# An attention and two-expert-layer kernel: `w_out`'s conversion, the gate products and the late logits placed later in attention, and the gate's weights loaded at another step

## The chip, the cores and the metric

The kernel runs on one core of a Trainium2 chip. The metric is the device time of one execution in microseconds (us); a smaller time is better. A core has a matrix engine (TensorE, PE in the profile, with its weight loads as PEld), a vector engine (VectorE, DVE), an activation engine (ScalarE, ACT), a general engine (GpSimd, POOL) and a queue engine (SyncE, SP) that issues most transfers. Each works through its own instructions in order and waits for the others by semaphores. Sixteen DMA engines move data between HBM and the on-chip memory.

## The reference, cut to what matters

Multi-head attention with normalized q and k, then a dense layer with an ELU between two matrices, then a layer of eight experts with a greedy assignment of tokens.

```python
# attention: 4 batches, 12 heads, 448 rows, 64 columns a head
q_n, k_n = rmsnorm(q, g_q), rmsnorm(k, g_k)
attn = softmax(scale * q_n @ k_n.T)
x = concat_heads(attn @ v)                 # 1792 x 768
# dense layer: w_in 768 x 2048, w_out 2048 x 768
h = x @ w_in
g = where(h > 0, h, exp(min(h, 0)) - 1)
x = g @ w_out
# experts: w_gate 768 x 8, w1 8 x 768 x 1024, w2 8 x 1024 x 768
logits = x @ w_gate
...                                        # greedy: best (token, expert) first, at most 224 a expert
for e in range(8):
    out[mask_e] = relu(x[mask_e] @ w1[e]) @ w2[e]
```

`w_in` and `w_out` come as 64-bit floats, the other inputs as 32-bit floats.

## The kernel before

Every product is made of 16-bit pieces: a matrix is split into a high and a low half, and three matmuls (high by high, low by high, high by low) stand for one. The logits must be exact enough to order the tokens, so they are not taken from `x @ w_gate` after the second matrix but from `g` by the product of `w_out` and `w_gate`, called `Wg` here, which the kernel makes itself.

Attention goes over 24 pairs of heads (4 batches of 6 pairs), two pairs (a `Duo`) being loaded, normalized and transposed together. For each pair PE makes scores (`ps`), DVE their maxima (`sm`), ScalarE the exponentials (`pe`), GpSimd scales them, PE transposes them (`pta`, `ptb`) and multiplies them by v (`po`); ScalarE and DVE then write the two halves of the result into `xT` (lines 578 and 579).

Beside attention run other streams of work. `w_in` is converted from 64-bit floats (`load_steps`, lines 369 to 383: three DVE operations into `cv`, two on ScalarE, one on GpSimd). The hidden layer of a finished batch (`hidden`, line 665) has 16 blocks of 18 matmuls (`ph`), each followed by the ELU and two stores of `g` to HBM (`g_d`, `gt_d`). `w_out` is converted in 16 blocks (`gate_products`, line 602): each block `wo` is stored to HBM (`wo_d`), transposed by two DMA transposes (`wt`), and PE multiplies it by the gate's weights (`pw`, 12 short matmuls), which gives 128 rows of `Wg`. The logits of batches 2 and 3 are made from `g` while it is on the chip; those of batches 0 and 1 (`late_logits`, line 653) need `g` from HBM again: four blocks of `g` are loaded into four buffers (`gl`), and PE adds their logits (`pl`, a group of 8 matmuls). After attention the hidden layer of the last batch and the second matrix (`py`) follow, with `w_out` loaded from `wo_d`, then the assignment of tokens, woven with the rest of the second matrix, and then the experts.

The order of the streams is written by time steps. A pair has 16 steps, so attention has 384 and its loads begin at step -48. `at(t, f)` puts a piece of attention at step t. A `Spread(gen, n, t0, t1)` takes n pieces from a generator at an even pace from step t0 to step t1. After that the framework's scheduler orders the instructions of each engine by its own estimate of time, from the dependencies and this order; the built order of both programs is therefore quoted below. The lines that the change touches are the last two spreads and the step of `load_gate`:

```python
Spread(gate_products(), NG, 180, 280),
Spread(chain_gens(late_logits(b) for b in range(LB)), 2 * LB * NF // LG, 295, 400),
...
at(-30, load_gate)
```

Names: `wg` are the gate's weights, `acc` the logits' sums, `st` the landing buffers of weights (three), `wo` has two buffers, `wt` three, `gl` four, and `pt` in PSUM has three that `pta`, `ptb`, `po`, `pw` and `pl` share.

Of the kernel before, what the change touches and what calls it, by code (L numbers as in the profile page):

```python
# [8 lines left out]
F16 = mybir.dt.float16  # L9
# [246 lines left out]
def kernel(  # L256
# [14 lines left out]
    nc = tc.nc  # L271
    PE, ACT, DVE, POOL = nc.tensor, nc.scalar, nc.vector, nc.gpsimd

    B, H, S, D = q.shape
# [5 lines left out]
    P = 128  # L280
    NP = H // 2
    KC = DM // P
    NF = FF // P
# [3 lines left out]
    MAIN = NJ * P  # L287
    TAIL = S - MAIN
# [33 lines left out]
    def mm(o, l, r, key=None, **kw):  # L322

        i = PE_mm(o, l, r, **kw)  # L324
        if key is not None:
            if key in last_in_bank:
                tc.add_manual_dep(i.ins, last_in_bank[key].name, NOSYNC, reason="order in a bank")
            last_in_bank[key] = i.ins
        return i
# [6 lines left out]
    g_d = [dram.tile([P, NF, 2, MAIN], F16, name=f"g_d{b}") for b in range(B)]  # L336

    gt_d = [dram.tile([P, NF, 2, 2 * TAIL], F16, name=f"gt_d{b}") for b in range(B // 2)]
# [18 lines left out]
    def load_steps(hi, lo, src):  # L357

        w = src.shape[1]
        if src.dtype == F32:  # L360
            st = stg.tile([P, w], F32, tag="st", name="st")
            i = nc.sync.dma_start(st, src)
            if hold:
                tc.add_manual_dep(i.ins, hold[-1].ins.name, NOSYNC, reason="not before its turn")
            split(hi, lo, st, w)
            yield
            return

        for a in range(0, w, 512):
            n = min(512, w - a)  # L370
            st = stg.tile([P, n, 2], I32, tag="st", name="st")
            nc.sync.dma_start(st.rearrange("p n t -> p (n t)"), src[:, a:a + n].bitcast(I32))
            cv = gat.tile([P, n], I32, tag="cv", bufs=3, name="cv")
            i = DVE.tensor_scalar(cv, st[:, :, 1], 3, 0x3FFFFFF8, op0=ALU.logical_shift_left, op1=ALU.bitwise_and)
            if pace:
                tc.add_manual_dep(i.ins, pace[-1].ins.name, NOSYNC, reason="not before its turn")
            DVE.scalar_tensor_tensor(cv, st[:, :, 1], -0x40000000, cv, op0=ALU.bitwise_and, op1=ALU.bitwise_or)  # L377
            DVE.scalar_tensor_tensor(cv, st[:, :, 0], 29, cv, op0=ALU.logical_shift_right, op1=ALU.bitwise_or)  # L378
            cf = cv.bitcast(F32)
            ACT.activation(cf, cf, AF.Copy, scale=SW)  # L380
            ACT.copy(hi[:, a:a + n], cf)
            POOL.tensor_sub(lo[:, a:a + n], cf, hi[:, a:a + n])
            yield
# [13 lines left out]
    def key():  # L397
        n_key[0] += 1
        return n_key[0]
# [4 lines left out]
    gat = att_s.enter_context(tc.tile_pool(name="gat", bufs=2))  # L404
# [3 lines left out]
    psT = ps1.enter_context(tc.tile_pool(name="psT", bufs=3, space=PSUM))  # L408
# [188 lines left out]
    def load_gate():  # L597
        nc.sync.dma_start(wg32, w_gate.rearrange("(c p) e -> p c e", p=P))
        ACT.activation(wg16[:, :, 0:NE], wg32, AF.Copy, scale=-SW)
        DVE.scalar_tensor_tensor(wg16[:, :, NE:], wg32, -SW, wg16[:, :, 0:NE], op0=ALU.mult, op1=ALU.subtract)  # L600

    def gate_products():
        wts = None
        for f in range(NF):
            wo = gat.tile([P, 2, DM], F16, name="wo")
            yield from load_steps(wo[:, 0, :], wo[:, 1, :], w_out[f * P:(f + 1) * P, :])
            if f:
                gate_product(f - 1, wts)
                yield
            nc.sync.dma_start(wo_d[:, f], wo)  # L610
            wts = []
            for z in range(2):
                wts.append(gat.tile([P, KC, P], F16, name="wt", bufs=3))
                nc.sync.dma_start_transpose(wts[z], wo[:, z, :])
            yield
        gate_product(NF - 1, wts)
        yield

    def gate_product(f, wts):
        pw = psT.tile([P, 2 * NE], F32, tag="pt", name="pw")  # L620
        for z in range(2):
            n = NE if z else 2 * NE
            for c in range(KC):
                mm(pw[:, 0:n], wts[z][:, c, :], wg16[:, c, 0:n], start=(z == 0 and c == 0),
                   stop=(z == 1 and c == KC - 1), skip_group_check=True)
        t = gat.tile([P, NE], F32, name="wgt")
        ACT.copy(t, pw[:, NE:])
        DVE.tensor_add(t, t, pw[:, 0:NE])
        DVE.tensor_copy(Wg[:, f, 0:NE], t)
        DVE.tensor_copy(Wg[:, f, WG:], t)  # L630
        DVE.tensor_sub(Wg[:, f, NE:2 * NE], t, Wg[:, f, 0:NE])

    LG = 4

    def logits(pool, tag, b, gs):

        pl = pool.tile([P, S], F32, tag=tag, name="pl")
        kk = key()
        for i, (g, f) in enumerate(gs):
            for z, (o, n) in enumerate(((0, WG), (WG, NE))):  # L640
                mm(pl[o:o + n], Wg[:, f, o:o + n], g[:, z, :], key=kk,
                   start=(i == 0), stop=(i == len(gs) - 1), skip_group_check=True)
        n = WG + NE
        for o, w, c in ((b * MAIN, MAIN, 0), (B * MAIN + b * TAIL, TAIL, MAIN)):
            a = acc[:, o:o + w]
            if gs[0][1] == 0:
                DVE.tensor_copy(a, pl[0:n, c:c + w])
            else:
                DVE.tensor_add(a, a, pl[0:n, c:c + w])

    LB = 2

    def late_logits(b):
        for f in range(0, NF, LG):
            gs = []
            for i in range(f, f + LG):
                gl = gat.tile([P, 2, S], F16, bufs=LG, name="gl")
                nc.sync.dma_start(gl[:, :, 0:MAIN], g_d[b][:, i])
                nc.sync.dma_start(gl[:, :, MAIN:S], gt_d[b // 2][:, i, :, b % 2 * TAIL:(b % 2 + 1) * TAIL])
                gs.append((gl, i))  # L660
            yield
            logits(psT, "pt", b, gs)
            yield

    def hidden(b, xT):

# [28 lines left out]
        if b >= LB:  # L695
            logits(psT, "pt", b, gs[NF - LG:NF])
# [14 lines left out]
    def chain_gens(gens):  # L711
        for g in gens:
            yield from g

    def w_in_steps(u):
        for c in range(KC):
            load_w_in(u, c)
            yield
# [5 lines left out]
    def at(t, f, *a):  # L724
        todo.setdefault(t, []).append((f, a))

    NG = NF * (2 + DM // 512 + 1)
    spreads = [
        Spread(w_in_steps(0), KC, 40, 96),
        Spread(chain_gens(w_in_steps(i) for i in range(1, FF // WB)), KC * (FF // WB - 1), 96, 176),  # L730
        Spread(gate_products(), NG, 180, 280),
        Spread(chain_gens(late_logits(b) for b in range(LB)), 2 * LB * NF // LG, 295, 400),
    ]
    at(-47, load_gain)
    at(-30, load_gate)
    NSTEP = B * SEQ
    for b in range(B):
        xT = big.tile([P, KC, 2, S], F16, name="xT")
# [122 lines left out]
    for o in range(0, NCH, h):  # L861
        pt = psR.tile([P, h, n], F32, tag=f"rt_pb{4 if o else 0}", name="plt")
# [152 lines left out]
```

## Time and profile before

| | |
|---|---|
| time, median of 3 runs | 1150.81 us (1146.79 to 1153.8) |
| the profiled execution | 1149.89 us, its span 1148.2 us |
| PE busy in the span | 1037.0 us (90%) |
| DVE | 787.0 us (69%) |
| ACT | 538.5 us (47%) |
| POOL | 354.1 us (31%) |
| mean granted TensorE clock | 0.968 of full speed |

The profile is one execution. Busy time is the time in which an engine had an instruction at work, so instructions that overlap are counted once, and a matmul that runs at the lower clock counts with its longer time. The share over the whole span is a mean over stages with different limits: attention ends about 540 us after the span's start, the second matrix and the assignment of tokens follow to about 880, then the experts. The table by stretch is the view that tells the stages apart.

### The profile page before, as it was taken

Reading aid. Unit: us, or ns where it says so; the run is one execution under the profiler, and the core shown is the slowest. Engines: PE = TensorE matmul, PEld = TensorE weight load, DVE = VectorE, ACT = ScalarE, POOL = GpSimd, SP = SyncE. Lnnn points to the kernel's source line nnn. Section 1 sums busy time; section 2 is a strip of 40 time slices with the busy share of each in tenths; the row PEclk is TensorE's granted clock in tenths of the full one; section 3 lists DMA queues with packets and bytes.
Section 4 is the critical chain, followed back from the end, with each engine's and each line's share of the span. In section 5 each row is a group of like instructions: output and inputs, shape, how many; then the busy total and the mean of one; then the engine's idle time right before and its main releaser. Section 6 shows DMA issues by size and latency. Waiting matters only on the chain.

```text
span 1148.2 us, 19348 instructions
## 1 busy us (share of the span) xinstructions
PE 1037.0 (90%) x7030; PEld 608.9 (53%) x7030; DVE 787.0 (69%) x1567; ACT 538.5 (47%) x1099; POOL 354.1 (31%) x462
## 2 busy tenths in 40 slices
PE   0687879897989989999999999999999799999997
PEld 0233434443544444444444545555546688888885
DVE  3798898999988775654334778887786556666620
ACT  2676677776867765554441111011112455555510
POOL 3677686657756542221001000000000412222100
PEclk9977889999999999999999999999999899999999
DMA  6355575559998736334922151131133778777710
GB/s 173 80 123 130 136 206 164 152 162 246 259 246 207 193 74 135 97 80 148 398 78 69 59 196 59 49 132 49 49 104 100 238 244 247 255 252 255 239 41 25
DMA packets 190319, 176.48 MB, mean 154 GB/s; under 512 B 114704, under 2 KB 161808, under 8 KB 189456
## 3 DMA queue, kind: packets, MB, share of 16 engines
q1 hardware_dynamic: 186064, 163.78, 49.7%
q0 software_dynamic: 3328, 11.01, 3.0%
q8 instruction: 55, 0.90, 0.3%
q10 hardware_dynamic: 832, 0.46, 0.1%
q14 instruction: 40, 0.33, 0.1%
HBM read 125.92 MB, written 31.98 MB: 138 GB/s over the span
## 4 chain that ended last, share of the span: by engine, by line
PE 51%; DVE 18%; DMA 11%; issue 10%; ACT 5%; POOL 3%; SPq 2%; POOLq 0%; DVEq 0%; ACTq 0%
PE py L324 18%; PE ph L324 11%; DMA st<-in_moe_w_dram 4%; PE pye L324 4%; PE po L324 4%; PE phe L324 3%; DVE sm L533 2%; PE ps L324 2%; PE rt_pc L324 2%; DVE cv L377 2%; PE pta L324 2%; DMA qn<-in_q_dram 2%; PE pl L324 1%; DVE cv L378 1%; DVE rt_C L127 1%
## 5 line engine op out<-in xcount | busy, mean ns | idle before, releaser
L324 PE MATMUL ph<-xT,w_in 128*128 128x448 f16 x1152 | 247.2, 359 | 7.8 <-DVE elu_g L685 4.8
L324 PE MATMUL py<-w_out,g 128*128 128x384 f16 x1152 | 203.8, 328 | 0.0
L324 PEld LDWEIGHTS <-w_in 128*128 128x128 f16 x1152 | 108.0, 99 | 125.4 <-issue 44.7
L545 POOL TENSOR_SCALAR pe<-pe,sm 128x448 f32<-128x448 f32 x168 | 127.0, 766 | 141.0 <-DVE sm L541 78.9
L351 DVE SCALAR_TENSOR_TENSOR w<-st,w 128x768 f16<-128x768 f32 (+1 forms) x112 | 119.4, 1073 | 72.1 <-ACT w L350 65.8
L324 PEld LDWEIGHTS <-g 128*128 128x128 f16 x1152 | 107.3, 98 | 81.4 <-issue 18.5
L350 ACT ACTIVATE w<-st 128x768 f16<-128x768 f32 (+1 forms) x112 | 103.8, 933 | 89.3 <-DMA st<-in_moe_w_dram 84.0
L324 PE MATMUL ps<-kT,qT 64*128 64x448 f16 (+1 forms) x576 | 94.3, 382 | 54.5 <-ACT pe L535 29.2
L535 ACT ACTIVATE pe<-ps,sm 128x448 f32<-128x448 f32 x168 | 105.7, 633 | 50.1 <-DVE sm L533 47.6
L324 PE MATMUL pye<-w,hT 128*112 128x512 f16 (+1 forms) x768 | 126.4, 326 | 0.0
L127 DVE TENSOR_SCALAR rt_C<-rt_row,rt_m 128x1792 f16<-128x1792 f32 x98 | 107.3, 1149 | 8.2 <-PE rt_pc L324 7.4
L533 DVE TENSOR_REDUCE sm<-ps 128x1 f32<-128x448 f32 x168 | 100.2, 614 | 17.8 <-PE ps L324 15.5
L324 PEld LDWEIGHTS <-w 128*128 128x128 f16 x1152 | 110.4, 99 | 3.3 <-DVE xTe L922 1.2
L324 PE MATMUL phe<-xTe,w 128*128 128x224 f16 x1080 | 109.2, 261 | 2.1 <-DVE xTe L922 1.1
L324 PEld LDWEIGHTS <-hT 128*112 128x112 f16 x768 | 91.6, 130 | 32.1
L815 ACT ACTIVATE xh<-py 128x384 f16<-128x384 f32 x28 | 13.7, 490 | 176.6 <-PE py L324 159.2
L324 PEld LDWEIGHTS <-qT 64*128 64x128 f16 (+1 forms) x576 | 27.5, 100 | 99.0 <-issue 65.9
L324 PE MATMUL pta<-id,pe 128*128 128x128 f32 x384 | 65.3, 293 | 12.7 <-POOL pe L545 4.7
L685 DVE SCALAR_TENSOR_TENSOR elu_g<-ph,elu_e 128x448 f32<-128x448 f32 x64 | 39.6, 618 | 48.0 <-ACT elu_e L683 47.7
L972 POOL DMA_INDIRECT out_dram<-yo,idx x16 | 18.5, 1155 | 173.9 <-DVE yo L971 172.3
L324 PEld LDWEIGHTS pta<-id,pe 128*128 128x128 f32 x384 | 46.1, 148 | 43.1 <-POOL pe L545 16.0
L201 POOL MEMSET rt_c<- 128x8 f16 x8 | 0.9, 123 | 210.1 <-DVE rt_c L207 206.0
(176 smaller groups left out, 1475.1 us busy)
## 6 DMA issues: line engine op xcount, KB each, us to landing
st<-in_moe_w_dram SPq DMA_DIRECT2D x48, 512.0 KB
st<-in_moe_w_dram SPq DMA_DIRECT2D x64, 384.0 KB
st<-in_moe_w_in_dram SPq DMA_DIRECT2D x24, 512.0 KB
g_d<-gt SPq DMA_DIRECT2D x64, 192.0 KB
g<-g_d SPq DMA_DIRECT2D x16, 768.0 KB
st<-in_moe_w_out_dram SPq DMA_DIRECT2D x16, 512.0 KB
gl<-g_d SPq DMA_DIRECT2D x32, 192.0 KB
wo_d<-wo SPq DMA_DIRECT2D x16, 384.0 KB
```

What stands on the lines that cost most here:

```text
L127: i = DVE.tensor_scalar(C.rearrange("p c t -> p (c t)"), row, m[:, s:s + 1], None, op0=ALU.is_le)
L324: i = PE_mm(o, l, r, **kw)
L350: ACT.activation(hi, st, AF.Copy, scale=SW)
L351: DVE.scalar_tensor_tensor(lo, st, SW, hi, op0=ALU.mult, op1=ALU.subtract)
L377: DVE.scalar_tensor_tensor(cv, st[:, :, 1], -0x40000000, cv, op0=ALU.bitwise_and, op1=ALU.bitwise_or)
L378: DVE.scalar_tensor_tensor(cv, st[:, :, 0], 29, cv, op0=ALU.logical_shift_right, op1=ALU.bitwise_or)
L533: i = DVE.tensor_reduce(out=st[:, 0, u:u + 1], in_=ps[u], axis=AX.X, op=ALU.max, negate=True)
L535: ACT.activation(p[:, u, :], ps[u], AF.Exp, bias=st[:, 0, u:u + 1], accum_out=st[:, 1, u:u + 1])
L545: POOL.tensor_scalar(p[:, u, :], p[:, u, :], st[:, 2, u:u + 1], 1.0, op0=ALU.mult, op1=ALU.mult)
L685: DVE.scalar_tensor_tensor(gf, ph, -SG / SH, e, op0=ALU.mult, op1=ALU.min)
L815: ACT.activation(xh[:, 0], py, AF.Copy, scale=-SX2 / (SG * SW))
L972: st = POOL.indirect_dma_start(out=out, out_offset=bass.IndirectOffsetOnAxis(ap=idx[:, 1, 2 * e + hh:2 * e + hh + 1], axis=0), in_=yo, in_ ...
```

## The change

The conversion of `w_out` with the gate products is spread over steps 240 to 368 in place of 180 to 280. The late logits are spread over steps 285 to 400 in place of 295 to 400, and their loop is turned: for each group of four blocks first batch 0, then batch 1, where before all groups of batch 0 came first. So logits are taken from a part of `Wg` while the rest is still being made; a list `ready` and an assertion, which cost nothing on the chip, hold that the order is right. `load_gate` moves from step -30 to step 100.

```diff
--- before.py
+++ after.py
@@ -599,13 +599,15 @@
         ACT.activation(wg16[:, :, 0:NE], wg32, AF.Copy, scale=-SW)
         DVE.scalar_tensor_tensor(wg16[:, :, NE:], wg32, -SW, wg16[:, :, 0:NE], op0=ALU.mult, op1=ALU.subtract)
 
+    ready = []
+
     def gate_products():
-        wts = None
         for f in range(NF):
             wo = gat.tile([P, 2, DM], F16, name="wo")
             yield from load_steps(wo[:, 0, :], wo[:, 1, :], w_out[f * P:(f + 1) * P, :])
             if f:
                 gate_product(f - 1, wts)
+                ready.append(f - 1)
                 yield
             nc.sync.dma_start(wo_d[:, f], wo)
             wts = []
@@ -614,6 +616,7 @@
                 nc.sync.dma_start_transpose(wts[z], wo[:, z, :])
             yield
         gate_product(NF - 1, wts)
+        ready.append(NF - 1)
         yield
 
     def gate_product(f, wts):
@@ -634,6 +637,7 @@
 
     def logits(pool, tag, b, gs):
 
+        assert gs[-1][1] in ready
         pl = pool.tile([P, S], F32, tag=tag, name="pl")
         kk = key()
         for i, (g, f) in enumerate(gs):
@@ -650,17 +654,18 @@
 
     LB = 2
 
-    def late_logits(b):
+    def late_logits():
         for f in range(0, NF, LG):
-            gs = []
-            for i in range(f, f + LG):
-                gl = gat.tile([P, 2, S], F16, bufs=LG, name="gl")
-                nc.sync.dma_start(gl[:, :, 0:MAIN], g_d[b][:, i])
-                nc.sync.dma_start(gl[:, :, MAIN:S], gt_d[b // 2][:, i, :, b % 2 * TAIL:(b % 2 + 1) * TAIL])
-                gs.append((gl, i))
-            yield
-            logits(psT, "pt", b, gs)
-            yield
+            for b in range(LB):
+                gs = []
+                for i in range(f, f + LG):
+                    gl = gat.tile([P, 2, S], F16, bufs=LG, name="gl")
+                    nc.sync.dma_start(gl[:, :, 0:MAIN], g_d[b][:, i])
+                    nc.sync.dma_start(gl[:, :, MAIN:S], gt_d[b // 2][:, i, :, b % 2 * TAIL:(b % 2 + 1) * TAIL])
+                    gs.append((gl, i))
+                yield
+                logits(psT, "pt", b, gs)
+                yield
 
     def hidden(b, xT):
 
@@ -728,11 +733,11 @@
     spreads = [
         Spread(w_in_steps(0), KC, 40, 96),
         Spread(chain_gens(w_in_steps(i) for i in range(1, FF // WB)), KC * (FF // WB - 1), 96, 176),
-        Spread(gate_products(), NG, 180, 280),
-        Spread(chain_gens(late_logits(b) for b in range(LB)), 2 * LB * NF // LG, 295, 400),
+        Spread(gate_products(), NG, 240, 368),
+        Spread(late_logits(), 2 * LB * NF // LG, 285, 400),
     ]
     at(-47, load_gain)
-    at(-30, load_gate)
+    at(100, load_gate)
     NSTEP = B * SEQ
     for b in range(B):
         xT = big.tile([P, KC, 2, S], F16, name="xT")
```

On ACT, at the start of the program (`sq` squares of q and k, `wg` the gate's weights, `ln` and `rs` the normalizing factors, `h` the cast halves, `pe` the first exponentials), before:

```order
L451 ACTIVATE sq<-qn 128x896
L599 ACTIVATE wg_99<-wg_98 128x6x8
L451 ACTIVATE sq<-kn 128x896
L459 ACTIVATE ln<-ss,eps 128x28
L461 ACTIVATE rs<-ln 128x28
L480 CAST h_180<-kn 128x896
L480 CAST h_186<-qn 128x896
L535 ACTIVATE pe,sm<-ps,sm 128x448
```

and changed:

```order
L451 ACTIVATE sq<-qn 128x896
L451 ACTIVATE sq<-kn 128x896
L459 ACTIVATE ln<-ss,eps 128x28
L461 ACTIVATE rs<-ln 128x28
L480 CAST h_177<-kn 128x896
L480 CAST h_183<-qn 128x896
L599 ACTIVATE wg_99<-wg_98 128x6x8
L535 ACTIVATE pe,sm<-ps,sm 128x448
```

The gate's weights moved from the second place to the one ahead of the first exponential.

On DVE, in a late pair of attention, before (`elu_g` and `gt` belong to the hidden layer, `acc` to the late logits):

```order
L533 TENSOR_REDUCE sm<-ps 128x1 x2
L685 SCALAR_TENSOR_TENSOR elu_g<-ph,elu_e 128x448
L540 TENSOR_SCALAR sm<-sm 128x2
L541 RECIPROCAL sm<-sm 128x2
L649 TENSOR_TENSOR acc<-acc,pl 40x384
L649 TENSOR_TENSOR acc<-acc,pl 40x64
L688 TENSOR_TENSOR gt<-elu_g,gt 128x448
L560 COPY PT<-ptb 128x3x128
```

and changed:

```order
L377 SCALAR_TENSOR_TENSOR cv<-st,cv 128x512
L579 SCALAR_TENSOR_TENSOR xT<-po,xT 128x448
L541 RECIPROCAL sm<-sm 128x2
L651 COPY acc<-pl 40x384
L651 COPY acc<-pl 40x64
L541 RECIPROCAL sm<-sm 128x1
L378 SCALAR_TENSOR_TENSOR cv<-st,cv 128x512
L533 TENSOR_REDUCE sm<-ps 128x1
L374 TENSOR_SCALAR cv<-st 128x256
L533 TENSOR_REDUCE sm<-ps 128x1
L560 COPY PT<-ptb 128x3x128
L377 SCALAR_TENSOR_TENSOR cv<-st,cv 128x256
```

The conversion's operations (`cv`) now stand among those of the late logits, which they had all left behind before.

On SP, around a group of loads of late logits, before:

```order
L440 DMA vn_4909<-in_v_dram 128x4x192
L658 DMA gl_5378<-g_d0_76 128x2x384
L659 DMA gl_5378<-gt_d0_80 128x2x64
L658 DMA gl_5381<-g_d0_76 128x2x384
L659 DMA gl_5381<-gt_d0_80 128x2x64
L658 DMA gl_5384<-g_d0_76 128x2x384
L689 DMA g_d2_78<-gt_5275 128x2x384
L690 DMA gt_d1_81<-gt_5275 128x2x64
```

and changed:

```order
L663 DMA gl_4462<-g_d1_77 128x2x384
L664 DMA gl_4462<-gt_d0_80 128x2x64
L612 DMA wo_d_84<-wo_4358 128x1536
L616 DMA_TRANSPOSE wt_4480<-wo_4358 128x6x128
L616 DMA_TRANSPOSE wt_4482<-wo_4358 128x6x128
L372 DMA st_4700<-in_moe_w_out_dram 128x1024
L372 DMA st_4730<-in_moe_w_out_dram 128x512
L372 DMA st_4854<-in_moe_w_out_dram 128x1024
L663 DMA gl_4757<-g_d0_76 128x2x384
L664 DMA gl_4757<-gt_d0_80 128x2x64
L663 DMA gl_4760<-g_d0_76 128x2x384
L616 DMA_TRANSPOSE wt_4662<-wo_4517 128x6x128
```

The store and the transposes of `wo` and the loads of `w_out` now share SP's order with the loads of late logits; before, only stores of `g` and loads of v stood between these.

## Rows read from the trace of the kernel before

**Rows 1.** ACT's copies into `xT`: start us, us; ends of pairs 9, 13, 16, 23.

```profile
235.89 0.54 ACT L578 ACTIVATE xT<-po 128x448 f16<-128x448 f32 x1
330.27 0.54 ACT L578 ACTIVATE xT<-po 128x448 f16<-128x448 f32 x1
407.19 0.53 ACT L578 ACTIVATE xT<-po 128x448 f16<-128x448 f32 x1
538.59 0.54 ACT L578 ACTIVATE xT<-po 128x448 f16<-128x448 f32 x1 [3.45 <-PE po L324]
```

**Rows 2.** Busy time of each engine in stretches A and B.

```profile
core 0: us, PE busy (x) PEld busy (x) DVE busy (x) ACT busy (x) POOL busy (x), PEclk, DMA share, GB/s
235.89:407.19 171.30, 152.95 (x1000) 76.18 (x999) 152.04 (x361) 123.62 (x302) 103.96 (x126) 0.97 0.88 222
407.19:538.59 131.40, 127.13 (x779) 61.99 (x780) 79.69 (x193) 74.61 (x182) 36.14 (x58) 1.00 0.39 93
```

**Rows 3.** PE's waits in stretch A: us in total, times, longest us.

```profile
PE ps L324 <- ACT pe L535: 8.5, 7, 3.2
PE pw L324 <- DMA wt<-wo: 1.1, 2, 0.8
```

**Rows 4.** PE's longest wait in stretch B.

```profile
PE ps L324 <- ACT pe L535: 1.8, 2, 1.1
```

**Rows 5.** The chain that ended last, in stretch A: transposes of `wo`.

```profile
335.90 5.14 DMA wt<-wo
...
360.83 3.58 DMA wt<-wo
...
388.89 2.45 DMA wt<-wo
```

**Rows 6.** Busy time by stretch: pairs 12, 13 and 14, 15, 16, and after attention.

```profile
280.48:303.92 23.44, 18.61 (x130) 10.12 (x130) 22.78 (x58) 16.05 (x42) 16.50 (x16) 0.85 0.99 253
303.92:359.69 55.77, 51.72 (x328) 24.93 (x327) 50.85 (x118) 41.06 (x101) 33.11 (x44) 0.97 0.97 250
359.69:383.50 23.81, 20.16 (x138) 10.49 (x138) 20.57 (x53) 18.60 (x47) 13.36 (x17) 1.00 0.73 191
383.50:407.19 23.69, 21.91 (x162) 11.40 (x159) 15.86 (x43) 14.73 (x37) 12.57 (x18) 1.00 0.83 180
540.00:560.00 20.00, 18.52 (x98) 8.67 (x97) 7.07 (x14) 8.78 (x15) 0.00 (x0) 1.00 0.98 406
```

**Rows 7.** The program's start in order of time: ScalarE, DVE and GpSimd.

```profile
11.44 0.23 DVE L315 SCALAR_TENSOR_TENSOR gain<-gain,gk_b 128x64 f32<-128x64 f32 x1 [1.58 <-DMA gk_b<-in_g_k_dram]
11.77 0.24 ACT L599 ACTIVATE wg<-wg 128x48 f16<-128x48 f32 x1 [3.03 <-DMA wg<-in_moe_w_gate_dram]
11.90 2.07 POOL L454 TENSOR_TENSOR qn<-qn,gain 128x896 f32<-128x896 f32 x1 [8.40 <-DMA vn<-in_v_dram]
11.92 0.95 ACT L451 ACTIVATE sq<-kn 128x896 f32<-128x896 f32 x1
12.04 1.99 DVE L600 SCALAR_TENSOR_TENSOR wg<-wg,wg 128x48 f16<-128x48 f32 x1 [0.38 <-ACT wg L599]
13.96 1.07 DVE L452 TENSOR_REDUCE ss<-sq 128x14 f32<-128x896 f32 x1
...
15.53 0.21 POOL L465 TENSOR_SCALAR ss<-ss 128x28 f32<-128x28 f32 x1 [1.56 <-ACT ln L459]
```

**Rows 8.** The chain that ended last: PE's pieces, start us, us, and their count.

```profile
357.74 0.39 PE pw L324 x12
...
538.54 1.62 PE pl L324 x15
...
549.57 3.52 PE ph L324 x18
...
565.17 0.93 PE py L324 x5
```

**Rows 9.** SP's longest wait in stretch B.

```profile
SPq L658 <- PE pl L324: 32.6, 8, 9.8
```

## The prediction

> **What bounds the kernel now.** I read the page first: its rows by slices show TensorE (PE) at nine tenths in most slices, so one has to look by stage. The moved work lies in attention, and I cut attention at the copies of its 24 head pairs into `xT`, counted from 0 [rows 1]. Pair 10 begins at 235.89 us, where conversion of `w_out` sets in; pair 16, the last that converts, ends at 407.19; the last pair ends at 538.59. The table of busy time by stretch [rows 2] then has two regimes. Stretch A (pairs 10 to 16, 171.30 us) has PE busy 152.95 us and VectorE (DVE) 152.04, both 89%, with the DMA engines at 0.88. Stretch B (pairs 17 to 23, 131.40 us) has PE busy 127.13 us, 97%, with DVE at 79.69 and DMA at 0.39. PE is idle 18.35 us in A (10.7%) and 4.27 us in B (3.2%). So B is bound by PE, and A by a mesh of DVE, DMA and PE. The waits say how A loses its time: PE's scores wait 8.5 us for ScalarE's exponentials in A [rows 3] and 1.8 in B [rows 4]; ScalarE and DVE work in order, and a conversion step that waits holds up what attention needs. The chain that ended last runs in A through the transposes of `wo` [rows 5], 2.5 to 5.1 us a time. Pair 12 stands out [rows 6]: 23.44 us, PE busy 18.61, granted clock 0.85.
>
> All of the possible gain in attention is therefore these 22.6 us of idle PE, and what the clock cost: A's mean is 0.97 against 1.00 in B, so some 3% of 152.95, 4.6 us, was lost at the lower of the two levels.
>
> **Start.** Before, ScalarE's second activation of the program waits 3.03 us for the gate's weights, ahead of the squares of `kn`, and on DVE the correction of these weights takes 1.99 us ahead of the sums of `kn` [rows 7]. The built order shows where they go: not to step 100, but just behind the first two casts of q and k, still ahead of the first exponential; the load goes behind three `w_in` loads on SP. So the words of the change promise more than the program does. DVE can start the sum of `kn` once `gain` is done at 11.67 rather than at 13.96, 2.3 us earlier. What is late next is GpSimd: its `qn` by `gain` ends at 13.97, and the Newton steps, which began at 15.53, can begin then: 1.6 us earlier. I take -1.6. Bounds: -2.3, if that product too runs faster without the DVE instruction beside it, and -0.5, if the correction (0.2 to 2 us on DVE) now delays the first maximum.
>
> **The bulk: pairs 10 to 23.** Up to the middle of pair 10 both programs have the same order on PE and DVE. I counted the instructions by pair in the two orders and gave them the pace of the chain [rows 8]: 3.52 us for 18 `ph`, 0.196 each; 0.39 us for 12 `pw`; 1.62 us for 15 `pl`. Stretch A holds 360 `ph` (70.4 us) and 192 `pw` (6.2); the other 76.3 us are attention, 10.9 a pair. Changed, pairs 10 to 13 hold 181 `ph` and no `pw`: 35.4 + 43.6 = 79.0 us of PE work. All of pairs 10 to 23 is 152.95 + 127.13 = 280.1 us plus 15 `ph` that the new order draws in from behind attention (2.9 us), 283.0. So 204.0 us are left for pairs 14 to 23, with all conversion, all products and seven of the eight groups of late logits.
>
> Pairs 10 to 13 resemble B: no conversion, DVE light. At B's 3.2% idle they last 79.0/0.968 = 81.6 us; before, with conversion and five `ph` more, they lasted 94.4, to 330.27 [rows 1]. For pairs 14 to 23 the idle share decides, and the trace has no such stretch. Nearest rows: B's 3.2% from below, A's 10.7% from above, and between them pairs 13 and 14 [rows 6], which are like the new pairs in having much PE work beside the conversion: 55.77 us, PE busy 51.72, 7.3% idle. I take 7.3%, the row that is nearest: 204.0/0.927 = 220.1 us. Two things speak for less than A: a block of `w_out` comes every 12 us of PE work instead of 9.6 (192.5 us in pairs 14 to 22, and 153, over 16 blocks), and DMA work of about 202 us (0.88 of 171.30 and 0.39 of 131.40) is spread more evenly. One speaks against: DVE's 231.7 us of both stretches less some 47 for pairs 10 to 13 (0.61, B's share, of 77) leaves 0.84 to 0.88 of the new stretch, nearly A's 0.89.
>
> Sum: 81.6 + 220.1 = 301.7 us against 302.70, so -1.0. Ends: 210.7 us at 3.2% gives -10.4; 228.4 us at 10.7% gives +7.3.
>
> **Tail.** The 15 `ph` are missing behind attention: -2.9 us. `w_out` comes back from HBM there, and the first product with it follows the last pair's end after 26.6 us [rows 8], now after some 23.6; the cover is the hidden layer's matmuls, and in 20 us of this load the queue moves 406 GB/s [rows 6], 8.1 MB, more than the 6.3 MB of `w_out` and the first part of `g`. I cost it at nothing; without that cover it is at most the same 2.9. Routing and experts have the same instructions. The late logits need `Wg` of their rows: the product that they need stands at least 13 us of PE work ahead, by the paces above, so I cost this at nothing too; if DVE were so far behind, the idle share above would hold it.
>
> **Clock.** Of the 4.6 us at the lower level I take back 2, since pairs 10 to 13 lose the idle stretches of A and pairs 14 on keep some. Bounds 0 and 4.6.
>
> **Forecast.** -1.6 - 1.0 - 2.9 - 2.0 = -7.5 us. The profiled execution took 1149.89 us around its span of 1148.2, 0.92 below the median of 1150.81. So 1142.4, and on the scale of the median 1143. Best ends together: -2.3 - 10.4 - 2.9 - 4.6 = -20.2, 1131. Worst: -0.5 + 7.3 - 2.9 = +3.9, 1155.
>
> **Rivals.** First, the idle time moves along with the conversion. 16 blocks cost what they cost, DVE's share stays near A's 0.89, and the new stretch idles 10.7% with no clock won: -1.6 + 7.3 - 2.9 = +2.8, 1153 or 1154 on the scale of the median, no change that can be measured. For it speaks that pairs 15 and 16 idle 11% together with a DVE that is not full (0.86 and 0.67) [rows 6]; against it, pairs 13 and 14. A's DMA share of 0.88 moved 222 GB/s, where the load behind attention moved 406 at 0.98. The Trainium skill, page "Perfetto Trace Analysis", section "Identifying the Most-Contended Engine", says to judge DMA by the bandwidth used and not by occupancy. By that rule DMA had room in A, its more even spread is worth nothing, and this rival's 1153 would be the sum rather than 1142; the trace's two bandwidths agree with the rule as far as they go. A's transfers are smaller and partly transposes, so its 222 GB/s may be all that these give, and I leave the rival below the forecast.
>
> Second, slower: SP becomes the wait. Before, the loads of late logits stood on SP alone with the stores of `g`, and SP waited 32.6 us in 8 times for PE to free their buffers [rows 9], 4.1 us each, costing nobody anything. Now the transposes and the store of `wo` and the next `w_out` loads stand behind such loads in five of seven groups. If each of these five waits goes through to PE's products and ScalarE's casts, it is 5 x 4.1 = 20 us on top of the forecast: 1163, slower. It decides once a wait exceeds the slack of a transpose, and the chain [rows 5] shows transposes with none. Against it: in the new order most of these loads stand behind the PE work that frees them, as the scheduler placed them, and their first reader comes 13 to 31 us of PE work later; only the last group has under 6.
>
> Third, more gain: pairs 14 to 23 run as B does, 3.2% idle: -1.6 - 10.4 - 2.9 - 2.0 = -16.9, 1134. For it speaks that B held late logits too and its longest wait of PE came to 1.8 us [rows 4]; against it, that DVE is at 0.61 there.
>
> **How the numbers follow.** Half a per cent, 5.75 us, is about what a measurement of this kernel can tell from no change. The forecast has 0.37, the third rival 0.15, both faster: 0.52. The first rival has 0.32, no change. The second has 0.14, and 0.02 are left for a later load of `w_out` or worse: slower 0.16. The range of 1131 to 1155 leaves out the second rival and little else.
>
> **What would show it.** In the new profile pair 10's end should come about 1.6 us earlier and pair 13's some 12 us earlier still; PE idle in pairs 10 to 13 near 3%, in pairs 14 to 22 near 7%; DVE's share there under 0.9. The first rival is right if PE idles a tenth in pairs 14 to 22 with DVE as the releaser; the second if SP waits for `pl` with transposes behind it and PE or ScalarE wait for `wt`. I am wrong in kind if attention's end comes more than 20 us earlier, or if time appears behind attention.

## The result and the profile after

The changed kernel took 1137.67 us, the median of 4 runs (1134.59 to 1140.95), beside 1151.24 for the kernel before; the ratio is 0.989, with a 95% interval of 0.984 to 0.993. A second set of runs gave 1138.7 us and 0.987 (0.983 to 0.991). So it is faster by a little over 1%, and 1143 with a range of 1131 to 1155 held it. The gain is 13.6 us between the medians, where 7.5 was forecast. The experiments below show that the gain hangs on something that the prediction did not have: the one order of instructions that was built.

The profiled execution took 1134.59 us around a span of 1132.7, 15.3 us below the profile before (15.5 between the spans). The ends of pairs 9, 13, 16 and 23, which answer to [rows 1] (start us, duration us, then ScalarE's copy into `xT`):

```profile
234.41 0.54 ACT L578 ACTIVATE xT<-po 128x448 f16<-128x448 f32 x1
308.18 0.54 ACT L578 ACTIVATE xT<-po 128x448 f16<-128x448 f32 x1
374.41 0.54 ACT L578 ACTIVATE xT<-po 128x448 f16<-128x448 f32 x1
528.17 0.54 ACT L578 ACTIVATE xT<-po 128x448 f16<-128x448 f32 x1 [4.22 <-PE po L324]
```

The pairs from 10 on now fall into 10 to 13, without conversion, and 14 to 23, with all of it; the third row is both together. It is the table of busy time by stretch, which answers to [rows 2]:

```profile
core 0: us, PE busy (x) PEld busy (x) DVE busy (x) ACT busy (x) POOL busy (x), PEclk, DMA share, GB/s
234.41:308.18 73.77, 73.32 (x420) 35.22 (x419) 52.42 (x111) 51.35 (x121) 37.85 (x52) 1.00 0.40 97
308.18:528.17 219.99, 209.49 (x1376) 103.46 (x1376) 182.26 (x445) 146.32 (x364) 103.42 (x132) 0.98 0.78 196
234.41:528.17 293.76, 282.81 (x1794) 138.68 (x1794) 234.68 (x554) 197.67 (x483) 141.27 (x183) 0.99 0.68 171
```

Where the 15.5 us of the span went: 1.5 by the end of pair 9 (235.89 to 234.41), 8.9 in pairs 10 to 23 (302.70 to 293.76), 5.1 behind them (604.5 us to the end of the span instead of 609.6). In pairs 10 to 23 PE's busy time is nearly what it was, 282.81 us against 280.08, though 15 `ph` more are in it; its idle time went from 22.6 to 10.95 us. Pairs 10 to 13 have next to none, 0.45 us. Pairs 19 and 20 run with PE never idle at a DMA share of 0.99 and 1.03 (a transfer counts in the stretch in which it starts, so a share can pass 1):

```profile
421.85:444.04 22.19, 22.19 (x152) 10.58 (x151) 20.45 (x52) 15.92 (x41) 10.84 (x15) 1.00 0.99 235
444.04:468.66 24.62, 24.62 (x167) 12.23 (x166) 17.96 (x49) 15.48 (x41) 8.21 (x13) 1.00 1.03 251
```

So a DMA share near 1.0, which pairs 11 to 14 had before (0.97 or more), need not hold PE up. That agrees with the rule that the prediction weighed (the Trainium skill, "Perfetto Trace Analysis", section "Identifying the Most-Contended Engine": bandwidth, not occupancy).

PE's longest waits in pairs 10 to 23 (us in total, times, longest), which answer to [rows 3, 4]:

```profile
PE ph L324 <- DVE elu_g L690: 3.5, 2, 2.7
PE pw L324 <- DMA wt<-wo: 2.2, 2, 1.4
PE ps L324 <- ACT pe L535: 1.4, 3, 0.6
```

The scores' wait for the exponentials, 8.5 us in stretch A alone, is down to 1.4. SP's wait for the late logits' buffers in pairs 14 to 23 answers to [rows 9], 8.8 us against 32.6:

```profile
SPq L663 <- PE pl L324: 8.8, 4, 5.3
```

On the chain that ended last one wait for a transpose of `wo` is left between the ends of pairs 13 and 23. Before there were four in stretch A, 13.9 us in all; [rows 5] shows three of them:

```profile
366.23 4.21 DMA wt<-wo
```

### The profile page after: what moved, and what is told of

The parts are those of the page before. It is cut to its first block, busy times and chain, and to the rows that moved or that the text cites. A ratio compares the mean times of both kernels' runs of the same rounds, so it can differ in the third digit from the quotient of the medians.

```text
span 1132.7 us, 19333 instructions
## 1 busy us (share of the span) xinstructions
PE 1031.3 (91%) x7030; PEld 607.0 (54%) x7030; DVE 786.6 (69%) x1567; ACT 538.8 (48%) x1099; POOL 352.3 (31%) x462
## 4 chain that ended last, share of the span: by engine, by line
PE 49%; DVE 16%; DMA 13%; issue 10%; ACT 5%; POOL 4%; SPq 2%; POOLq 0%; DVEq 0%; ACTq 0%
PE py L324 17%; PE ph L324 14%; DMA st<-in_moe_w_dram 8%; PE po L324 5%; PE ps L324 3%; DVE w L351 2%; PE rt_pc L324 2%; PE pta L324 2%; DVE sm L533 2%; ACT w L350 2%; DVE cv L377 1%; DMA qn<-in_q_dram 1%; PE pl L324 1%; DVE rt_C L127 1%; PE pye L324 1%
## 5 line engine op out<-in xcount | busy, mean ns | idle before, releaser
L545 POOL TENSOR_SCALAR pe<-pe,sm 128x448 f32<-128x448 f32 x168 | 130.2, 785 | 119.9 <-DVE sm L541 43.7
L127 DVE TENSOR_SCALAR rt_C<-rt_row,rt_m 128x1792 f16<-128x1792 f32 x98 | 107.3, 1150 | 8.2 <-PE rt_pc L324 7.4
L533 DVE TENSOR_REDUCE sm<-ps 128x1 f32<-128x448 f32 x168 | 100.5, 615 | 12.2 <-PE ps L324 11.7
L324 PE MATMUL pta<-id,pe 128*128 128x128 f32 x384 | 65.8, 295 | 13.9 <-DVE xT L579 4.2
L324 PEld LDWEIGHTS pta<-id,pe 128*128 128x128 f32 x384 | 47.1, 149 | 44.6 <-POOL pe L545 17.5
```

What stands on the lines that cost most here:

```text
L127: i = DVE.tensor_scalar(C.rearrange("p c t -> p (c t)"), row, m[:, s:s + 1], None, op0=ALU.is_le)
L533: i = DVE.tensor_reduce(out=st[:, 0, u:u + 1], in_=ps[u], axis=AX.X, op=ALU.max, negate=True)
L545: POOL.tensor_scalar(p[:, u, :], p[:, u, :], st[:, 2, u:u + 1], 1.0, op0=ALU.mult, op1=ALU.mult)
```

## The experiments

Two questions were put first. Is the gain due to the late **place**, where VectorE has less other work, or to the slower **pace** (16 blocks over 128 steps instead of 100)? And does VectorE bound the stretch with the conversion? The answers raised a third: how much of the gain belongs to the one **order of instructions** that the scheduler built.

All runs in one table (us): the ratio is from all executions of a run, the other columns are from the one that was profiled. "Rest" is from the end of pair 23 to the end of the span; "wt" is the time in which PE and ScalarE, in pairs 10 to 23, waited for transposes of `wo`.

| run | conversion at steps | pairs 10-13 | pairs 14-23 | PE idle, 10-23 | rest | wt: PE + ACT | ratio to before (95%) |
|---|---|---|---|---|---|---|---|
| before | 180-280 | 94.4 | 208.3 | 22.6 | 609.6 | 1.1 + 4.7 | 1 |
| after | 240-368 | 73.8 | 220.0 | 10.9 | 604.5 | 2.2 + 0 | 0.989 (0.984-0.993) |
| after again | 240-368 | 73.8 | 220.0 | 11.7 | 604.5 | 2.2 + 0 | 0.987 (0.983-0.991) |
| early, dense | 180-280 | 96.4 | 210.8 | 23.4 | 612.4 | 0 + 5.7 | 1.000 (0.997-1.002) |
| late, dense | 262-362 | 74.4 | 236.7 | 22.3 | 606.0 | 2.6 + 3.7 | 1.000 (0.997-1.002) |
| early, slow | 180-308 | 95.6 | 212.1 | 22.0 | 611.4 | 3.6 + 12.6 | 1.003 (1.000-1.005) |
| late, slower | 220-368 | 79.4 | 221.9 | 15.6 | 608.7 | 1.9 + 0.8 | 0.992 (0.989-0.995) |
| two paces | 232-288-368 | 74.3 | 232.2 | 19.5 | 611.8 | 4.4 + 4.5 | 0.999 (0.997-1.001) |
| 4 steps earlier | 236-364 | 73.8 | 234.9 | 20.2 | 610.6 | 7.9 + 15.8 | 1.003 (1.000-1.006) |
| 4 steps later | 244-372 | 73.5 | 234.8 | 19.7 | 606.3 | 5.3 + 14.9 | 0.999 (0.996-1.001) |
| later, faster | 248-372 | 74.3 | 231.8 | 17.5 | 603.8 | 6.1 + 4.8 | 1.001 (0.999-1.003) |
| less VectorE | 180-280 | 94.5 | 217.3 | 25.5 | 609.2 | 5.5 + 19.5 | 1.006 (1.003-1.009) |
| less GpSimd | 180-280 | 98.8 | 212.1 | 25.2 | 611.0 | 2.9 + 3.0 | 1.008 (1.005-1.010) |
| gate weights alone | 180-280 | 95.9 | 207.4 | 22.7 | 607.5 | 1.5 + 4.3 | 1.000 (0.997-1.004) |

### Place and pace

The changed kernel again, and three placements that undo one side of the change at a time.

> The changed kernel unchanged, so that the next three stand beside it on one chip. Every theory: the same as in its first runs, about 13 us below the kernel before (ratio 0.989), profiled span near 1132.7 us, pairs 10 to 13 in 73.8 us and pairs 14 to 23 in 220.0.

```diff
-        Spread(gate_products(), NG, 240, 368),
+        Spread(gate_products(), NG, 180, 280),
```

> The changed kernel with the conversion of w_out and the products back at steps 180 to 280; the turned order of the late logits (from step 285) and the later gate weights stay. Place theory (the gain comes from conversion having left the pairs in which VectorE still has Duo halves and PE has only attention): pairs 10 to 16 take about 171 us again with PE idle some 18 us, and the kernel is 1.5 to 3 us below the kernel before, the gain at the start and a little in the logits. Rival that the order of the late logits carries the gain: 8 us or more below the kernel before, with pairs 17 to 23 shorter than 131.4 us.

```diff
-        Spread(gate_products(), NG, 240, 368),
+        Spread(gate_products(), NG, 262, 362),
```

> The changed kernel with the conversion at steps 262 to 362: late, but at the old pace of 100 steps. Place theory: about as fast as the changed kernel, 12 to 18 us below the kernel before, PE idle in pairs 10 to 23 about 8 to 12 us. Pace theory (the gain comes from 16 blocks over 128 steps instead of 100, which leaves each transpose and buffer more time): PE idle again about 18 to 22 us, and only 3 to 7 us below the kernel before.

```diff
-        Spread(gate_products(), NG, 240, 368),
+        Spread(gate_products(), NG, 180, 308),
```

> The changed kernel with the conversion at steps 180 to 308: early, at the new pace of 128 steps. Place theory: pairs 10 to 17 lose PE time as before, 14 to 20 us idle, and the kernel is 2 to 5 us below the kernel before. Pace theory: idle falls to about 10 us, and it is 10 to 14 us below.

The changed kernel repeats itself: the same stretches within 0.03 us, the same idle time within 1. The early, dense conversion is as slow as before, so the new order of the late logits and the later gate weights, which this run keeps, bring nothing by themselves. But neither place nor pace alone brings anything either: late and dense idles 22.3 us, early and slow 22.0. Both theories failed their own run. Late and dense shows what a crowded pair looks like. A block of `w_out` is converted in two pieces, 512 and 256 wide, called half blocks here. In pair 17 of this run six half blocks meet the last halves of q and k; VectorE has no gap and PE idles 10 us:

```profile
380.73:409.13 28.40, 18.32 (x110) 8.11 (x111) 28.32 (x62) 17.63 (x45) 23.57 (x26) 0.88 0.77 202
```

### VectorE's and GpSimd's load, taken away

In the kernel before, for `w_out` alone, one VectorE operation of each half block is left out, or GpSimd's subtraction becomes a ScalarE copy. Either leaves a part of `w_out` out of the result.

```diff
-            DVE.scalar_tensor_tensor(cv, st[:, :, 0], 29, cv, op0=ALU.logical_shift_right, op1=ALU.bitwise_or)
+            if w != DM:
+                DVE.scalar_tensor_tensor(cv, st[:, :, 0], 29, cv, op0=ALU.logical_shift_right, op1=ALU.bitwise_or)
```

> The kernel before with the third VectorE operation of the conversion left out for w_out (its three lowest mantissa bits are left out of the result): 32 operations of 0.42 or 0.68 us, some 18 us of VectorE's busy time in pairs 10 to 16, while every transfer stays. Theory that PE idles there because of VectorE: pairs 10 to 16 shrink from 171.3 us by 6 to 14, PE's 18 us of idle time to 6 to 12. Rival that the DMA engines hold the stretch: by 2 us or less.

```diff
-            POOL.tensor_sub(lo[:, a:a + n], cf, hi[:, a:a + n])
+            if w == DM:
+                ACT.copy(lo[:, a:a + n], cf)
+            else:
+                POOL.tensor_sub(lo[:, a:a + n], cf, hi[:, a:a + n])
```

> The kernel before with GpSimd's subtraction in the conversion of w_out replaced by a third ScalarE copy (w_out's low half is left out of the result: a copy of the high value stands there): 32 operations of about 1.36 us leave GpSimd. VectorE's conversion steps took 55 us in pairs 10 to 16, and 46 at their shortest durations; the long ones stand beside work of GpSimd. Theory that this meeting of the two engines is part of the loss: the steps fall to 50 us or less and pairs 10 to 16 shrink by 3 to 8 us. Rival that it isn't, and that only VectorE's own work counts: within 2 us of 171.3.

Both made the kernel slower, which no theory had. In pairs 10 to 16 VectorE's busy time fell from 152.04 us to 134.66 in the first and 144.76 in the second, GpSimd's in the second from 103.96 to 68.63, and yet these pairs grew from 171.3 us to 179.0 and 177.7. The row of the run with less VectorE work:

```profile
233.34:412.37 179.03, 157.32 (x1000) 76.70 (x999) 134.66 (x329) 122.84 (x303) 99.54 (x126) 0.94 0.88 212
```

The row of the run with less GpSimd work:

```profile
232.74:410.45 177.71, 155.11 (x998) 75.65 (x997) 144.76 (x361) 136.01 (x334) 68.63 (x94) 0.96 0.90 214
```

What grew in the first is ScalarE's wait for the transposes of `wo`, 4.7 us before and 19.5 here, by the waits of ScalarE in these pairs:

```profile
ACT wo L382 <- DMA wt<-wo: 19.5, 7, 5.6
```

In the second, VectorE is still busy 53.9 us with conversion steps, against 52.8 before. The theory that the meeting with GpSimd is part of the loss wanted these steps shorter; they were not, so this run does not settle it. These two are no clean test of a load. The scheduler orders instructions by its own estimates of their durations, so taking an operation away rebuilt the order: of 1,567 VectorE records in the trace some 290 in the one and 270 in the other stand at another place in the sequence. They do show that less work on VectorE was no gain in these two orders, and they put the wait on `wt` forward.

### Levelling the load

```diff
-        Spread(gate_products(), NG, 240, 368),
+        Spread(gate_products(), NG, 220, 368),
```

> The changed kernel with the conversion at steps 220 to 368, 9.25 steps a block instead of 8. In the first runs neither late and dense nor early and slow was faster than before, only late and slow. Theory of the level load (PE idles in the pairs in which VectorE's load with conversion passes PE's work): 3.5 instead of 4 halves a pair in pairs 15 to 18 take some 1 us a pair off, two more pairs pay up to 1 each; 0 to 4 us faster than the changed kernel, PE idle in pairs 10 to 23 at 7 to 11 us. Theory of the place alone: 1 to 3 us slower.

```diff
-        Spread(gate_products(), NG, 240, 368),
+        Spread(gp, 5 * NG // NF, 232, 288),   # gp = gate_products()
+        Spread(gp, NG - 5 * NG // NF, 288, 368),
```

> The changed kernel with the conversion at two paces: 5 blocks at steps 232 to 288 (11.2 steps each, while VectorE still makes Duo halves), 11 blocks at 288 to 368 (7.3 each). Theory of the level load: PE's idle time in pairs 15 to 18 falls from 9.6 us to 3 to 6, pairs 19 to 22 stay without any, and the kernel is 3 to 8 us faster than the changed kernel. If pairs 19 to 22 have no room for 4.4 halves each, they idle 3 us or more and nothing is won.

The slower spread over steps 220 to 368 keeps most of the gain, 0.992, but at 1142.5 us it does not beat the changed kernel, as the theory of the level load wanted, and PE idles 15.6 us where 7 to 11 was expected. That is nearer to the theory of the place alone, slower by 1 to 3 us. The two paces, built to take load off just the pairs that idled, lose all of the gain: 6.6 us idle in pair 17, 3.1 in pair 19, 2.9 in pair 21. The level load was not tested cleanly by this, though. The steps asked for the first ten half blocks at 2.9 a pair, over 3.5 pairs; in the trace VectorE begins 4, 4, 3, 5, 4, 4, 6, 2 in pairs 14 to 21, so the first ten take less than three. The order that was built had not taken the load off.

### Neighbours of the changed kernel

If a run that was built to be better lands at 0.999, the changed kernel may owe its time to its one order. So the same change a quarter of a pair earlier, a quarter of a pair later, and half a pair later in its start:

```diff
-        Spread(gate_products(), NG, 240, 368),
+        Spread(gate_products(), NG, 236, 364),
```

> The changed kernel with the conversion at steps 236 to 364: the same pace, a quarter of a pair earlier. Theory that late place and slow pace as such carry the gain: 1133 to 1143 us, pairs 10 to 23 in 291 to 299. Rival that much of it is the particular order of instructions that the scheduler built for 240 to 368: then this order, which differs in its details, lands anywhere between 1138 and 1153, with pairs 10 to 23 up to 307 us.

```diff
-        Spread(gate_products(), NG, 240, 368),
+        Spread(gate_products(), NG, 244, 372),
```

> The changed kernel with the conversion at steps 244 to 372: the same pace, a quarter of a pair later. Place and pace: 1133 to 1142 us, pairs 10 to 23 in 290 to 298. Rival of the particular order: anywhere between 1138 and 1153, on the other side of the first from its neighbour as likely as not.

```diff
-        Spread(gate_products(), NG, 240, 368),
+        Spread(gate_products(), NG, 248, 372),
```

> The changed kernel with the conversion at steps 248 to 372, 7.75 steps a block. Over the nine profiles so far a pair from 10 to 18 with 1 to 4 halves loses 2.3 us of PE time on average, one from 19 to 22 0.8: by these means half a pair fewer early is 1 us less idle, so 1133 to 1140 us if the means hold. Rival of the particular order: 1138 to 1153.

The rival of the particular order is right, and even it was too hopeful for the first neighbour (1154.49 us where it went up to 1153, and 308.6 where it went up to 307). In the table of steps place and pace are the same within a quarter of a pair, and the gain is gone on either side: 1.003 and 0.999, with pairs 10 to 23 in 308.6 and 308.3 us instead of 293.8. The third, at 1150.44 us, shows that the means over pairs, from which 1133 to 1140 was expected, do not foretell an order. Pairs 10 to 13 are as good as ever in all three (73.5 to 74.3 us); all of it is lost in pairs 14 to 23. The row of the first neighbour against the second row of after above:

```profile
307.65:542.51 234.86, 215.12 (x1376) 104.53 (x1376) 177.95 (x445) 146.45 (x363) 104.53 (x132) 0.95 0.76 183
```

The same number of PE instructions, 1376, is recorded. 9.2 us more are idle, and 5.6 us more are busy: the mean granted clock there is 0.95 against 0.98.

**One loss, followed.** In this neighbour PE's and ScalarE's longest waits in pairs 10 to 23 are for the transposes of `wo`; after had 2.2 us of the first and none of the second. PE's:

```profile
PE pw L324 <- DMA wt<-wo: 7.9, 4, 3.7
```

ScalarE's:

```profile
ACT wo L381 <- DMA wt<-wo: 15.8, 5, 5.7
```

The longest of both is one event, at 440 us. First SP's queue in order of time (start us, duration us, what is issued; `SPq` is SP's DMA queue), with the transposes of k and q for the last two pairs in front:

```profile
436.57 4.01 SPq L490 DMA_TRANSPOSE kT<-h  x2
440.64 2.92 SPq L490 DMA_TRANSPOSE qT<-h  x2
443.65 1.24 SPq L616 DMA_TRANSPOSE wt<-wo  x1
444.99 0.53 SPq L694 DMA_DIRECT2D g_d<-gt  x1
```

Four transposes keep the queue for 7.1 us, and a transpose of `wo` stands behind them. It needed a `wt` buffer that PE's product of the block before freed at 438.1 us; from then on only the queue's order held it, for 5.5 us. PE has the product of that block in its own order. It does the first half, and then may do nothing else (PE's row by time):

```profile
442.55 0.30 PE L324 MATMUL pw<-wg,wt 128*128 128x16 f16 x6
446.53 0.31 PE L324 MATMUL pw<-wg,wt 128*128 128x8 f16 x6 [3.68 <-DMA wt<-wo]
```

ScalarE stands too: its cast into `wo` waits for the same transposes to have read that buffer, of which there are two, and behind the cast stand the exponentials of attention (ScalarE's rows by time):

```profile
446.55 0.62 ACT L381 CAST wo<-cv 128x512 f16<-128x512 f32 x1 [5.74 <-DMA wt<-wo]
447.08 0.56 ACT L692 CAST gt<-elu_g 128x448 f16<-128x448 f32 x1
447.55 0.63 ACT L535 ACTIVATE pe<-ps,sm 128x448 f32<-128x448 f32 x1
```

And the idle time is paid twice. In stretches of 2 us, PE's busy time is the first number behind the length, and the granted clock the number ahead of the DMA share:

```profile
444.00:446.00 2.00, 0.00 (x0) 0.00 (x0) 0.00 (x0) 0.00 (x0) 0.16 (x1) 1.00 0.89 168
446.00:448.00 2.00, 1.47 (x10) 0.73 (x11) 0.33 (x1) 1.45 (x3) 0.75 (x1) 0.66 0.81 187
448.00:450.00 2.00, 2.00 (x6) 0.60 (x4) 2.00 (x5) 1.42 (x6) 0.41 (x1) 0.50 0.73 146
```

PE stood for nearly 4 us, and the granted clock then is at the lower of its two levels, 1.2 GHz, until 450: PE is busy all of 448 to 450 and gets through half the work, so the stop of 3.7 us costs some 1.5 us more (half of 2.00, and a third of the 1.47 before).

In the changed kernel the same four transposes of k and q are in SP's order with a transpose of `wo` between them:

```profile
426.38 2.99 SPq L490 DMA_TRANSPOSE kT<-h  x2
429.46 1.24 SPq L616 DMA_TRANSPOSE wt<-wo  x1
430.79 0.53 SPq L372 DMA_DIRECT2D st<-in_moe_w_out_dram  x1
431.37 1.23 SPq L490 DMA_TRANSPOSE qT<-h  x1
```

PE's product that needs the one at 429.46 comes 7 us later and waits for nothing:

```profile
436.58 0.46 PE L324 MATMUL pw<-wg,wt 128*128 128x16 f16 x12
```

**What is shown and what isn't.** That the order decides is shown: the same change a quarter of a pair off in the table of steps, to either side, loses all of the gain. That a transpose of `wo` behind other transposes on SP stops PE and ScalarE is shown in this one place. That such stops are most of the difference is only argued: in the table the two fast orders (three profiles) have 2.2 to 2.7 us of `wt`, the eleven other profiles 5.7 to 25.0, but the amount does not follow the idle time (late and dense idles 22.3 us with 6.3 of `wt`). No run took that wait away with the order held, and a third buffer for `wo` wasn't tried.

Two other things set the changed kernel apart, and no run separates them from it. The scores' wait for the exponentials in pairs 10 to 23, 1.4 and 1.0 us in its two profiles, is 3.3 to 6.8 us in the six other late orders, the slower spread among them. In the first neighbour:

```profile
PE ps L324 <- ACT pe L535: 6.5, 7, 1.4
```

And equal steps are not an equal pace in the order that is built. The half blocks that VectorE begins in pairs 14 to 21 are 3, 4, 4, 5, 4, 4, 4, 4 in the changed kernel, 5, 6, 4, 4, 4, 4, 4, 1 in the neighbour 4 steps earlier, 2, 6, 5, 4, 4, 2, 5, 4 in the one 4 steps later and 0, 8, 4, 4, 3, 5, 5, 3 in the third. So an even spread on VectorE remains a rival to the transposes. Against it: the two paces are nearly as even up to pair 19 and idle 14.9 us in pairs 14 to 19, where the changed kernel idles 9.3, and pair 17 of the changed kernel, with five half blocks and VectorE busy 24.65 of 26.54 us, idles only 1.4.

### The gate's weights alone

```diff
-    at(-30, load_gate)
+    at(100, load_gate)
```

> The kernel before with the load of the gate's weights alone moved to step 100: in the built order nothing else moves. The seven profiles so far with the later weights begin the Newton steps at 13.65 to 14.62 us against 15.38 to 15.53 in the three without, but end pair 9 at 232.7 to 234.6 against 232.7 to 235.9. Theory that the start is worth 1 to 1.5 us to the end: pairs 10 to 23 in about 302.7 us as before, pair 9's end near 234.4, the kernel 1 to 2 us faster. Rival that it is lost again before pair 10: Newton steps near 14, the time within 1 us of before.

The Newton steps begin at 13.58 us, where they began at 15.53 [rows 7] and, in the changed kernel, at 14.30. GpSimd's row of this run:

```profile
13.58 0.21 POOL L465 TENSOR_SCALAR ss<-ss 128x28 f32<-128x28 f32 x1
```

The same row of after:

```profile
14.30 0.21 POOL L465 TENSOR_SCALAR ss<-ss 128x28 f32<-128x28 f32 x1
```

Pair 9 ends at 234.62. The whole kernel's ratio is 1.000 (0.997 to 1.004), its median 1148.91 us beside 1151.45: a gain of the expected size is neither shown nor excluded. Over all profiles pair 9 ends at 232.7 to 236.1 with the later weights (11 profiles, mean 234.4) and at 232.7 to 235.9 without (3, mean 234.0). Against the 15.53 us of before, the Newton steps begin 0.8 to 2.0 us earlier in these, and nothing of it can be seen 220 us later.

## Why the prediction was right in number, and where it was wrong

- **Start, -1.6.** The first profile shows 1.5 at pair 9. The mechanism is right at its place: VectorE's sum of `kn` begins at 11.83 us instead of 13.96, 2.1 earlier (2.3 was said), and the Newton steps 1.2 earlier (1.6 was said). But the other profiles say that it is not there by pair 9, within a scatter of 3.4 us. The 1.5 agreed by chance.
- **Pairs 10 to 23 together.** The two terms below hold 283.0 us of PE work and 18.7 us of idle time. Measured are 282.8 and 10.95. So the sum of the work was right, and what the forecast missed here, for this one order, is idle time.
- **Pairs 10 to 13, 81.6 us.** They took 73.8, and 73.5 to 74.4 in every order that has no conversion in them. The term was too long in both its factors. PE's work here is 73.3 us instead of 79.0. A part of this is a wrong count: the trace of before has 372 `ph` and 180 `pw` in stretch A, not 360 and 192, which at the prediction's own paces leaves some 74.3 us for attention, 10.6 a pair instead of 10.9. Another part fell behind pair 13: 85 matmuls of scores are in these pairs, where before had 99. And the idle share is 0.6%, not 3.2%. Of the 20.6 us by which these pairs are shorter than before, 10.3 are busy time of PE, most of it work that is now done later; the other 10.3 are idle time that is gone, and that is the one part that place alone gives.
- **Pairs 14 to 23, 220.1 us.** After shows 219.99, by two misses that cancel, which is luck: PE busy 209.5 instead of 204.0, since what was too much in the term before was missing here, and 4.8% idle instead of 7.3%. This is the weakest step of the prediction. It took an idle share from the nearest row as if it were a property of the stretch, and set 228.4 us as its far end. The other orders with the conversion from pair 14 or 15 on took 231.8 to 236.7, beyond that end: they idle 7.3 to 9.2%, and PE's busy time is 213 to 216 us at a mean granted clock of 0.95 to 0.96, against 0.98 in the changed kernel.
- **Clock, -2.** Over the span the sign is right: a mean of 0.974 against 0.968. But the 2 us were to come out of PE's busy time in pairs 10 to 23, and that is 279.9 us without the 15 `ph` (2.9 us), against 280.1 before; the second profile has 279.2. For the neighbours the sign is wrong too: 0.963 to 0.965 over the span.
- **Tail, -2.9.** Measured -5.1. Over the eight profiles with late conversion behind pair 13 or so, the rest of the span is 607.0 us on average, over the six with early conversion 610.2: 3.2 less, near the term. The remaining 2 us of after come and go: 603.8 to 611.8 among the late orders.
- **The first rival**, that the idle time moves along with the conversion, for 1153 or 1154. It fell for the changed kernel. But it is nearly what five of the seven late placements did: 20 us gained in pairs 10 to 13, 23 to 28 given back from pair 14 on, between 2 lost and 6 won behind, and a time of 1150 to 1154. Their new stretch idles less than the 10.7% that this rival set, and pays the rest in PE's busy time. Its chance of 0.32 was too small for the change as an idea; that the built order could decide between it and the forecast had no place among the rivals.
- **The second rival**, SP waiting for `pl` with transposes behind it, fell: 8.8 us against 32.6. Its mechanism, transposes of `wo` held up on SP, is the loss that was followed in the first neighbour, but there transposes of k and q stand in front, not the late logits' loads.

No other order beat the changed kernel; the nearest is the slower spread at 1142.5 us.

## What to carry to other kernels

Where a scheduler builds the order from a table of steps, one run of a new step measures one order: time its neighbours (a few steps earlier and later) before you put a gain down to the idea, and keep the best order as an order. In such a stretch look first for in-order queues on which a transfer that a matmul waits for stands behind others that nobody needs yet; here four transposes on SP cost PE 3.7 us at once and some 1.5 us more by the clock. An idle share read from a neighbouring stretch is no safe term of a sum: here 7.3% was set, and the late orders idled 4.8 to 9.2% in that stretch.

## What the hardware showed that was not expected

In the rows above a transpose holds SP's queue for 1.2 us, and two of them in a row for 2.9 to 4.0 us; in the changed kernel the median of its 80 transposes is 1.26 us, that of its 557 ordinary loads and stores 0.44. The first conversion step of a piece 512 wide, of `w_in` or `w_out`, took VectorE 0.41 us in most cases but up to 2.1 in others; in the late, dense run these are two of them:

```profile
383.89 1.26 DVE L374 TENSOR_SCALAR cv<-st 128x512 int32<-128x512 int32 x1
...
398.31 0.41 DVE L374 TENSOR_SCALAR cv<-st 128x512 int32<-128x512 int32 x1
```

GpSimd was busy in both, with the product of q and the gain beside the long one and with the scaling of exponentials beside the short one:

```profile
382.79 2.08 POOL L454 TENSOR_TENSOR qn<-qn,gain 128x896 f32<-128x896 f32 x1
...
396.98 2.16 POOL L545 TENSOR_SCALAR pe<-pe,sm 128x448 f32<-128x448 f32 x2 [0.30 <-DVE sm L541]
```

The long one ends at 385.15 us, 0.28 us after GpSimd's product. That is the rule in the traces: the twelve profiles in which no operation was taken away hold 480 such steps, and of the 113 that took over 0.7 us, 112 end 0.27 to 0.31 us after the GpSimd instruction that was running when they began. The 159 with no GpSimd instruction beside them took 0.40 to 0.44 us. It reads as VectorE standing until GpSimd is done. The short step above does not fit this: GpSimd's instruction beside it begins 0.05 us earlier by the trace and ends later. 33 of the 480 end like it before the GpSimd instruction that was running.

Taking work off VectorE or GpSimd made the kernel slower by 0.6 and 0.8%, both beyond their intervals.
